# An attention and two MLPs on one core: the first weights' splits ranked among the second attention's units, and half of the fifth block's result moved out of the buffer rings

## The chip, the cores and the metric

The kernel runs on one core of a Trainium2 chip. The metric is the time of one execution on the device in microseconds (us). Three runs of the kernel before gave a median of 1018.32 us (1017.8 to 1019.97).

## What is computed

A block-causal attention (4 batches, 8 heads, 576 positions, 64 values per head; a position sees all positions of its own block of 64 and of the blocks before), whose output, 2304 tokens by 512, goes through two multilayer perceptrons of the same size:

```python
def _attn_ref(q, k, v):
    scores = scale * np.matmul(q, k.transpose(0, 1, 3, 2))
    mask = block_i >= block_j
    scores = np.where(mask, scores, -1000000000.0)
    scores = scores - np.max(scores, axis=-1, keepdims=True)
    attn = np.exp(scores)
    attn = attn / (np.sum(attn, axis=-1, keepdims=True) + 1e-09)
    return np.matmul(attn, v)

def _moe_ref(x, w_in, w_out):      # 512 -> 2048 -> 512
    h = x @ w_in
    g = np.maximum(0.01 * h, h)
    return g @ w_out

def _moe2_ref(x, w_in, w_out):     # 512 -> 2048 -> 512
    h = x @ w_in
    g = h * (1.0 / (1.0 + np.exp(-h)))
    return g @ w_out
```

All inputs and outputs are 4-byte floats; the weights reach the kernel as 8-byte floats and are converted on the chip.

## The kernel before, in words

The tokens are cut into six blocks of 384. The attention of block b+1 is computed while the first MLP of block b runs, so that TensorE always has matmuls of the MLP to do. The second MLP follows, in nine blocks of 256 tokens, each in pairs of hidden chunks, and its first weights are converted and split during the last layer blocks.

**One layer block** has 16 steps f (NF), one for each 128 of the 2048 hidden units: a first half H (h, into PSUM; L1114 in block 0, L1119 to L1121 later), the gate (leaky relu, ScalarE, L1167), and a second half A that adds to four chunks of PSUM, acc (L1131 in block 0, L1139 later). In the text, H31 is the first half of step 31, counted over all blocks: block 0 has steps 0 to 15, block 1 has 16 to 31, and so on. Block 0 takes the weights as plain 4-byte floats (4 matmuls per half). From block 1 on each factor is split in a high and a low part of the faster type fp32r, and three products are added (12 matmuls per half). For that each first weight is split once: ScalarE copies the high part (L296, w<-wx) and VectorE or GpSimd subtracts it to get the low one (L312, w<-wx,w). Likewise the gate's result is split at each step into ghi (L296) and glo (L312).

**The attention** is made of units (one head, 128 queries or some tails): scores s (TensorE, L833 or L838), the row maximum (VectorE, L845 or L847), the exponential p (ScalarE, L855), the norm (L862 to L865), the high part hl (L869) and the low part (VectorE, L874), a transposing DMA pt<-hl (L882), the value products x (TensorE, L896 to L898), and the output's way out of PSUM: a half by ScalarE (L721), the sum by VectorE (L727), and a split into xhi and xlo.

**What sets the order.** Nothing is ordered by hand. The class Schedule is a list scheduler that runs while the program is built: each piece of work is a task with the engines that may do it (and a cost in ns on each), the tasks it depends on, and a rank. An engine that comes free in the planner's own clock takes the ready task of lowest rank, and the tasks are written out on each engine in that order; on the chip, each engine then runs its list as it stands. A layer step has rank 16 blk + f; work that TensorE waits for is put ahead by GATE (−1000) or SHORT (−500). The conversion of the first weights (convert(), L326) ranks from 10.5 on, the units of attention 1 from 11 on, those of attention 2 some 75 to 92, the splits of the first weights (split_weights(), L401) as below:

```python
ts = split(DM, lambda d=d: d["x"], parts, deps, step_of(1, f) - LEAD + i % 2, ...)   # L423
```

With LEAD 2.0 that is 14 + f. From f = 5 on, a split's result lies in space that the keys and queries of attention 1 use until its last scores are done, so these splits depend on all of them.

convert() turns 8-byte floats into 4-byte ones: a load (SP, L337), a copy scaled by ScalarE into a buffer cy (L344), the low words into a buffer cc by ScalarE (L352) or VectorE (L354), a sign (VectorE, L357), a shift (VectorE, L361) and a sum (L366, VectorE or GpSimd). The loads land in the ring wraw. The same three rings of buffers, wraw, cy and cc, also take the results of the layer blocks: when the last second half of a block is done, its four chunks of acc are copied out of PSUM (ScalarE L296 or VectorE L298, y<-acc) and stored to memory (yT<-y, SP, L1226). Which ring each chunk takes is set for each block by YRINGS ("r" wraw, "y" cy, "c" cc, "w" a place among the second weights):

```python
YRINGS = ("ryry", "crcr", "crcr", "crcr", "cycy", "wwww")
```

A buffer that holds a chunk comes free when its store has landed. The second MLP's weights are split into tiles of a pool "late" (LATE tiles, L1245), which takes the place of the attention's buffers when the attention has ended, and the planner adds the weights that don't fit as earlier steps come free.

Of the kernel before, what the change touches and what calls it, by code (L numbers as in the profile page):

```python
# [19 lines left out]
P = 128  # L20
# [6 lines left out]
NB2 = 256  # L27
FAST = 5
SEQ = 576
LATE = 10  # L30
NATIVE = 15
WARM = 11
LEAD = 2.0
LOAD0 = -1000
TURN = 0
COLD = 1.2
# [4 lines left out]
START0, START1 = -42.0, -26.0  # L41
STEP2 = 1.2
W2_BEFORE, W2_FIRST, W2_SECOND = 6, 30, 32
YRINGS = ("ryry", "crcr", "crcr", "crcr", "cycy", "wwww")
W2_AHEAD = 22
KQR, KR, QR, VR = 960, 1728, 2048, 1792
PR, HLR, PTR = 1408, 2304, 2304
# [165 lines left out]
def attn_mlp_mlp(  # L213
# [50 lines left out]
    def act(n, psum=False, pointers=0):  # L264
        return 0.833 * n + (52 if psum else 94) + 93 * pointers
# [7 lines left out]
    def dve2x(n, pointers=0):  # L273
        return Both(0.521 * n + 68 + 61 * pointers)

    def pool(n):
        return Both(2.35 * n + 100)
# [48 lines left out]
    def convert(src, f, sl, rk, load_rank, to=None):  # L326

        d = {}  # L330
        raw_free, raw_after, raw_users = raws.next()
        cy_free, cy_after, cy_users = cys.next()
        cc_free, cc_after, cc_users = ccs.next()

        def load():
            r = raw.tile([P, DM], I64, tag="wraw", name="wraw")
            nc.sync.dma_start(out=r, in_=src[f, :, sl])  # L337
            d["w0"] = r.bitcast(U32).rearrange("p (n two) -> p n two", two=2)[:, :, 0]
            d["sign"] = r.bitcast(U16).rearrange("p (n four) -> p n four", four=4)[:, :, 3]
            d["top"] = r.bitcast(F32).rearrange("p (n two) -> p n two", two=2)[:, :, 1]  # L340

        def scaled(e):
            d["y"] = cy.tile([P, DM], F32, tag="cy", name="cy")
            nc.scalar.activation(d["y"], d["top"], AF.Copy, scale=2.0**-112)  # L344

        def half_words(i):
            return d["c"].bitcast(U16).rearrange("p (n two) -> p n two", two=2)[:, :, i]

        def low(e):
            d["c"] = cc.tile([P, DM], U32, tag="cc", name="cc")  # L350
            if e == "ACT":
                nc.scalar.activation(half_words(0), d["w0"], AF.Copy, scale=2.0**-29)  # L352
            else:
                nc.vector.tensor_scalar(half_words(0), d["w0"], 2.0**-29, None, op0=ALU.mult)  # L354

        def signed(e):
            nc.vector.tensor_scalar(half_words(1), d["sign"], 0x8000, None, op0=ALU.bitwise_and)  # L357

        def shifted(e):
            yu = d["y"].bitcast(U32)  # L360
            nc.vector.tensor_scalar(yu, yu, 3, None, op0=ALU.logical_shift_left)  # L361

        def added(e):
            ci = d["c"].bitcast(I32)
            d["x"] = d["c"].bitcast(F32) if to is None else to
            engine[e].tensor_tensor(d["x"].bitcast(I32), d["y"].bitcast(I32), ci, op=ALU.add)  # L366

        t_load = dma(raw_free, load_rank, DM * P * 8, load, after=raw_after)
        raws.takers.append(t_load.issue)
        t_y = plan.add({"ACT": act(DM)}, [t_load, *cy_free], rk, scaled, cy_after)  # L370
        cys.takers.append(t_y)
        t_w = plan.add({"DVE": dve2x(DM), "ACT": act(DM)}, [t_load, *cc_free], rk, low, cc_after)
        ccs.takers.append(t_w)
        t_c = plan.add({"DVE": dve2x(DM)}, [t_load], rk, signed, [t_w])
        t_t = plan.add({"DVE": dve2x(DM)}, [t_y], rk, shifted)
        t_x = plan.add(on_vector(DM), [t_w, t_c, t_t], rk, added)
        raw_users += [t_y, t_w, t_c]
        cy_users.append(t_x)
        if to is not None:
            cc_users.append(t_x)  # L380
        return d, t_x, cc_users
# [808 lines left out]
    def add_second(s):  # L1190
# [10 lines left out]
        y_there[blk] = []  # L1201
        for c in range(NC):
            kind = YRINGS[blk][c]
            if kind == "w":
                free, after, users = (), (), []
            else:
                turns = {"r": raws, "c": ccs, "y": cys}[kind]
                free, after, users = turns.next()
            d = {}

            def evac(e, c=c, d=d, kind=kind):
                if kind == "w":
                    if c % 2 == 0:
                        late_y.append(slot1(F32, "yl"))
                    y = late_y[-1][:, c % 2 * DM : (c % 2 + 1) * DM]
                elif kind == "r":
                    y = raw.tile([P, DM], I64, tag="wraw", name="y").bitcast(F32)
                elif kind == "c":
                    y = cc.tile([P, DM], U32, tag="cc", name="y").bitcast(F32)
                else:  # L1220
                    y = cy.tile([P, DM], F32, tag="cy", name="y")
                d["y"] = y[:, :n]
                copy(e, d["y"], s.acc[c][:, :n])
# [1 line left out]
            def store(c=c, d=d):  # L1225
                nc.sync.dma_start(out=yT[blk][:, c, :], in_=d["y"])  # L1226

            if kind == "w":
                after = y_order[-1:]
            t = plan.add(copy_on(n, True), [s.t_g2, *free], GATE + rk, evac, after)  # L1230
            if kind == "w":
                y_order.append(t)
            else:
                turns.takers.append(t)
# [427 lines left out]
```

## Time and profile before

| what | before |
|---|---|
| median of 3 runs | 1018.32 us (1017.8 to 1019.97) |
| profiled execution, its own time | 1017.75 us |
| profiled execution, its span | 1016.0 us |
| TensorE (PE) busy | 981.6 us |
| VectorE (DVE) busy | 762.7 us |
| ScalarE (ACT) busy | 577.2 us |
| GpSimd (POOL) busy | 196.3 us |
| mean granted TensorE clock | 0.992 |

The span is from the first to the last instruction of the profiled execution; its own time is 1.75 us more. PE is TensorE's matmuls, PEld its weight loads, which run beside them, SP the engine that issues the DMAs. The granted clock has two levels, 2.4 GHz (1.00) and 1.2 GHz (0.50); a mean between them says how much of a stretch had which.

### The profile page before, as it was taken

Reading aid. Unit: us, or ns where it says so; the run is one execution under the profiler, and the core shown is the slowest. Engines: PE = TensorE matmul, PEld = TensorE weight load, DVE = VectorE, ACT = ScalarE, POOL = GpSimd, SP = SyncE. Lnnn points to the kernel's source line nnn. Section 1 sums busy time; section 2 is a strip of 40 time slices with the busy share of each in tenths; the row PEclk is TensorE's granted clock in tenths of the full one; section 3 lists DMA queues with packets and bytes.
Section 4 is the critical chain, followed back from the end, with each engine's and each line's share of the span. In section 5 each row is a group of like instructions: output and inputs, shape, how many; then the busy total and the mean of one; then the engine's idle time right before and its main releaser. Section 6 shows DMA issues by size and latency. Waiting matters only on the chain.

```text
span 1016.0 us, 18148 instructions
## 1 busy us (share of the span) xinstructions
PE 981.6 (97%) x6417; PEld 862.8 (85%) x6417; DVE 762.7 (75%) x1891; ACT 577.2 (57%) x1398; POOL 196.3 (19%) x287
## 2 busy tenths in 40 slices
PE   7899999999899999999999999999999999999998
PEld 4656557999799999999999898888989889898897
DVE  6888879687978878877647999976666667666564
ACT  5886768676667666666545668643333333333332
POOL 3173438112130114112203124510000000000000
PEclk9999999999799999999999999999999999999999
DMA  8757772565664656568434445410010100000000
GB/s 266 247 148 179 193 146 71 116 147 111 143 143 117 132 134 123 114 138 191 112 62 135 145 146 176 125 43 22 22 42 1 43 1 22 22 1 22 1 22 22
DMA packets 159451, 102.64 MB, mean 101 GB/s; under 512 B 131456, under 2 KB 143744, under 8 KB 159360
## 3 DMA queue, kind: packets, MB, share of 16 engines
q1 hardware_dynamic: 159360, 101.48, 39.6%
q8 instruction: 50, 0.82, 0.3%
q14 instruction: 41, 0.34, 0.1%
HBM read 67.37 MB, written 9.44 MB: 76 GB/s over the span
## 4 chain that ended last, share of the span: by engine, by line
PE 51%; DVE 3%; DMA 2%; ACT 1%; issue 1%; POOL 0%; SPq 0%; DVEq 0%; POOLq 0%; ACTq 0%
PE h L1332 13%; PE acc L1455 11%; PE acc L1471 7%; PE h L1333 6%; PE acc L1139 6%; PE h L1119 2%; PE h L1121 2%; PE h L1120 2%; PE s L838 1%; DMA wraw<-w 1%; DMA yT<-y 1%; DMA pt<-hl 1%; PE x L896 0%; DMA kqr<-kq_l 0%; PE x L898 0%
## 5 line engine op out<-in xcount | busy, mean ns | idle before, releaser
L1139 PE MATMUL acc<-ghi,w 128*128 128x384 f32 x640 | 164.2, 337 | 1.9 <-ACT ghi L296 1.2
L1344 ACT ACTIVATE xlo<-xlo 128x256 f32<-128x256 f32 x144 | 59.6, 414 | 139.1 <-DVE xlo L1341 139.0
L1332 PE MATMUL h<-xhi,w 128*128 128x512 f32 x352 | 132.0, 398 | 0.0
L1341 DVE TENSOR_REDUCE xlo<-h 128x256 f32<-128x512 f32 x144 | 99.3, 690 | 37.1 <-PE h L1333 34.8
L1139 PEld LDWEIGHTS acc<-ghi,w 128*128 128x128 f32 x640 | 114.0, 188 | 3.3 <-ACT ghi L296 1.5
L1119 PE MATMUL h<-xhi,w 128*128 128x384 f32 x320 | 109.7, 343 | 0.3 <-ACT g L1167 0.3
L1120 PE MATMUL h<-xlo,w 128*128 128x384 f32 x320 | 107.6, 336 | 0.0
L1139 PE MATMUL acc<-glo,w 128*128 128x384 f32 x320 | 107.4, 336 | 0.2 <-DVE glo L312 0.2
L1121 PE MATMUL h<-xhi,w 128*128 128x384 f32 x320 | 107.5, 336 | 0.0
L855 ACT ACTIVATE p<-s,st 128x288 f32<-128x288 f32 (+5 forms) x144 | 73.4, 512 | 47.9 <-DVE st L847 35.2
L1333 PE MATMUL h<-xhi,w 128*128 128x256 f32 x352 | 98.9, 281 | 0.0
L312 DVE TENSOR_TENSOR g<-xlo,xhi 128x256 fp32r<-128x256 f32 x136 | 61.4, 452 | 40.0 <-ACT xhi L296 39.6
L874 DVE SCALAR_TENSOR_TENSOR hl<-p,st,hl 128x576 f16<-128x576 f32 (+6 forms) x120 | 80.4, 674 | 14.5 <-ACT hl L869 11.5
L296 ACT ACTIVATE xhi<-xlo 128x256 fp32r<-128x256 f32 x144 | 59.0, 415 | 48.8 <-PE acc L1455 29.1
L1332 PE MATMUL h<-xlo,w 128*128 128x512 f32 x224 | 85.5, 398 | 0.0
L869 ACT ACTIVATE hl<-p,st 128x576 f16<-128x576 f32 (+7 forms) x111 | 65.8, 596 | 25.9 <-DVE st L865 7.2
L896 PE MATMUL x<-pt,v 128*128 128x128 f16 (+1 forms) x432 | 70.7, 214 | 9.4 <-DMA pt<-hl 4.1
L1332 PEld LDWEIGHTS h<-xhi,w 128*128 128x128 f32 x352 | 66.3, 188 | 13.7
L1167 ACT ACTIVATE g<-h 128x384 f32<-128x384 f32 x96 | 46.6, 485 | 48.1 <-PE h L1121 44.8
L897 PE MATMUL x<-pt,v 128*128 128x128 f16 (+1 forms) x432 | 68.6, 212 | 0.0
L1471 PE MATMUL acc<-w,xhi 128*128 128x512 f32 (+1 forms) x225 | 67.5, 384 | 0.0
L1333 PEld LDWEIGHTS h<-xhi,w 128*128 128x128 f32 x352 | 66.6, 189 | 1.0
(147 smaller groups left out, 2514.4 us busy)
## 6 DMA issues: line engine op xcount, KB each, us to landing
wraw<-w SPq DMA_DIRECT2D x64, 512.0 KB, 4.5
kqr<-kq_l SPq DMA_DIRECT2D x16, 480.0 KB, 4.0
v<-vL SPq DMA_DIRECT2D x32, 160.0 KB, 3.5
out<-o SPq DMA_DIRECT2D x18, 256.0 KB, 2.0
yT<-y SPq DMA_DIRECT2D x20, 192.0 KB, 2.3
kqr<-kq_l SPq DMA_DIRECT2D x8, 416.0 KB, 3.5
kqr<-kq_l SPq DMA_DIRECT2D x8, 384.0 KB, 3.5
yr<-yT SPq DMA_DIRECT2D x6, 512.0 KB, 4.0
```

Source lines behind the costliest of these rows:

```text
L855: nc.scalar.activation(p[:rows, k0:k1], u.s[i][:rows, :w], AF.Exp, bias=nm[:rows], accum_out=s2[:rows, i : i + 1])
L874: nc.vector.scalar_tensor_tensor(hl[:rows, 1, :n], p[:rows], rc[:rows], hl[:rows, 0, :n], op0=ALU.mult, op1=ALU.subtract)
L896: nc.tensor.matmul(g.x[:, o], a, hi, start=j == 0, stop=False)
L1119: nc.tensor.matmul(h, w1_lo[s.f][:, sl], hi[:, c, : s.n], start=c == 0, stop=False)
L1120: nc.tensor.matmul(h, w1_hi[s.f][:, sl], lo[:, c, : s.n], start=False, stop=False)
L1121: nc.tensor.matmul(h, w1_hi[s.f][:, sl], hi[:, c, : s.n], start=False, stop=c == NC - 1)
L1139: nc.tensor.matmul(s.acc[c][:, : s.n], a, b, start=s.f == 0 and i == 0, stop=s.f == NF - 1 and i == 2)
L1332: nc.tensor.matmul(o, whi[:, sl], x, start=c == 0, stop=end, skip_group_check=True)
L1333: nc.tensor.matmul(o[:, :NB2], wlo[:, sl], x[:, :NB2], start=False, stop=end, skip_group_check=True)
L1341: nc.vector.tensor_reduce(place(2 * j, 2), both, axis=AX.X, op=ALU.add)
L1455: nc.tensor.matmul(o, a, b, start=bank not in seen, stop=end and j == 2, skip_group_check=True)
L1471: nc.tensor.matmul(o[:, c], a, b[:, c], start=False, stop=end, skip_group_check=True)
```

## The change

Four things are edited. The splits of the first weights rank 16 + f + 55 (+ 0 or 1) in place of 16 + f − 2, that is 71 + f and up. The planner's costs of the five operations of convert() are raised by 50 to 150 ns, and the sum's entry gets a cost of its own for VectorE. Chunks 0 and 1 of the fifth block's result (block 4) go to a new tile "y4" of the pool late, that is free from the end of the attention on, rather than to a buffer of cc and of cy; chunks 2 and 3 stay in cc and cy. The pool late has nine tiles for weights rather than ten.

```diff
-LATE = 10
+LATE = 9
...
-LEAD = 2.0
+LEAD = -55.0
...
-YRINGS = ("ryry", "crcr", "crcr", "crcr", "cycy", "wwww")
+YRINGS = ("ryry", "crcr", "crcr", "crcr", "llcy", "wwww")
...
-        t_y = plan.add({"ACT": act(DM)}, [t_load, *cy_free], rk, scaled, cy_after)
+        t_y = plan.add({"ACT": act(DM) + 50}, [t_load, *cy_free], rk, scaled, cy_after)
...
-        t_w = plan.add({"DVE": dve2x(DM), "ACT": act(DM)}, [t_load, *cc_free], rk, low, cc_after)
+        t_w = plan.add({"DVE": dve2x(DM) + 110, "ACT": act(DM) + 150}, [t_load, *cc_free], rk, low, cc_after)
...
-        t_c = plan.add({"DVE": dve2x(DM)}, [t_load], rk, signed, [t_w])
-        t_t = plan.add({"DVE": dve2x(DM)}, [t_y], rk, shifted)
-        t_x = plan.add(on_vector(DM), [t_w, t_c, t_t], rk, added)
+        t_c = plan.add({"DVE": dve2x(DM) + 110}, [t_load], rk, signed, [t_w])
+        t_t = plan.add({"DVE": dve2x(DM) + 60}, [t_y], rk, shifted)
+        t_x = plan.add({"DVE": dve(DM) + 70, "POOL": pool(DM)}, [t_w, t_c, t_t], rk, added)
...
-            if kind == "w":
-                free, after, users = (), (), []
+            if kind in "lw":
+                free, after, users = [end_of_attention] if kind == "l" else (), (), []
...
+                if kind == "l":
+                    if c % 2 == 0:
+                        late_y.append(late().tile([P, 2 * DM], F32, tag="y4", name="y4", bufs=1))
+                if kind in "lw":
                     y = late_y[-1][:, c % 2 * DM : (c % 2 + 1) * DM]
```

Since the planner decides the order, the whole order moves, on all engines. Three places follow.

The first is ScalarE in the last steps of layer block 0. `w<-wx` are copies for the first weights' splits; `g<-h` is the gate of a layer step, `k<-kqr` and `q<-kqr` belong to heads of attention 2, `p,st<-s,st` is an exponential, `hl<-p,st` a high part, `x<-x` a half of the attention's output on its way out. Before:

```order
L296 ACTIVATE w<-wx 128x512 x2
L1167 ACTIVATE g<-h 128x384
L296 ACTIVATE w<-wx 128x512 x3
L721 ACTIVATE x_1684<-x 64x128 x2
L296 ACTIVATE w<-wx 128x512 x3
L721 ACTIVATE x_1684<-x 64x64 x2
L296 ACTIVATE k<-kqr 128x576
L855 ACTIVATE p,st<-s,st 128x320
L296 ACTIVATE w<-wx 128x512
L296 ACTIVATE xhi<-x_1684 128x192
L1167 ACTIVATE g<-h 128x384
L296 ACTIVATE w<-wx 128x512 x3
```

After:

```order
L721 ACTIVATE x_1675<-x 64x128 x2
L869 ACTIVATE hl<-p,st 128x320
L855 ACTIVATE p,st<-s,st 128x448
L296 ACTIVATE w<-wx 128x512 x2
L721 ACTIVATE x_1675<-x 64x64 x2
L665 ACTIVATE q<-kqr 128x384
L296 ACTIVATE w<-wx 128x512
L296 ACTIVATE xhi<-x_1675 128x192
L869 ACTIVATE hl<-p,st 128x448
L296 ACTIVATE w<-wx 128x512
L855 ACTIVATE p,st<-s,st 128x288 x2
L1167 ACTIVATE g<-h 128x384
```

The copies for the splits now stand in ones and twos among work of attention 2, where it was twos and threes with one key and one exponential among them.

The second is TensorE at the turn from layer block 1 to 2, between A30 and H32. Before, 128 rows of attention stand there without a layer half; this is a piece of them, the end of one unit's values, three scores, and the start of the next values:

```order
L896 MATMUL x<-pt,v 128x64
L897 LDWEIGHTS v
L897 MATMUL x<-pt,v 128x64
L898 LDWEIGHTS v
L898 MATMUL x<-pt,v 128x64
L838 MATMUL s<-k,q 128x256 x2
L838 MATMUL s<-k,q 128x384 x2
L838 MATMUL s<-k,q 128x128 x2
L896 LDWEIGHTS v
L896 MATMUL x<-pt,v 128x128
```

After, the end of the attention between H31 and A30, A30 itself, and the first of the values behind it:

```order
L898 LDWEIGHTS v
L898 MATMUL x<-pt,v 128x128
L838 MATMUL s<-k,q 128x384 x2
L1139 MATMUL acc<-ghi,w 128x384 x2
L1139 MATMUL acc<-glo,w 128x384
L1139 MATMUL acc<-ghi,w 128x384 x2
L1139 MATMUL acc<-glo,w 128x384
L1139 MATMUL acc<-ghi,w 128x384 x2
L1139 MATMUL acc<-glo,w 128x384
L1139 MATMUL acc<-ghi,w 128x384 x2
L1139 MATMUL acc<-glo,w 128x384
L896 LDWEIGHTS v
```

Between two layer halves there is now one part of a unit's values and a score or two. Counted over the whole order, the first scores of attention 2 moved from behind H18 to behind H14.

The third is ScalarE at the turn from layer block 4 to 5; `y<-acc` is a chunk of the fifth block's result, `cy<-wraw` the first step of a conversion, `w<-cc` a copy for a split of the second weights. Before:

```order
L296 ACTIVATE y<-acc 128x384 x2
L1167 ACTIVATE g<-h 128x384
L296 ACTIVATE y<-acc 128x384
L296 ACTIVATE ghi<-g 128x384
L344 ACTIVATE cy<-wraw 128x512 x2
L1167 ACTIVATE g<-h 128x384
L296 ACTIVATE w_6700<-cc 128x512
L296 ACTIVATE ghi<-g 128x384
```

After:

```order
L296 ACTIVATE ghi<-g 128x384
L296 ACTIVATE y_6692<-acc 128x384 x2
L296 ACTIVATE y<-acc 128x384
L344 ACTIVATE cy<-wraw 128x512
L1167 ACTIVATE g<-h 128x384
L296 ACTIVATE ghi<-g 128x384
L344 ACTIVATE cy<-wraw 128x512
L1167 ACTIVATE g<-h 128x384
L296 ACTIVATE ghi<-g 128x384
L296 ACTIVATE w_6604<-cc 128x512
```

The first two chunks go to the new tile, all three of ScalarE's chunks stand behind one gate, and ghi comes ahead of the copy for a split.

## Rows read from the trace of the kernel before

**Rows 1.** First page: busy time by engine; busy tenths and clock in 40 slices.

```profile
PE 981.6 (97%) x6417; PEld 862.8 (85%) x6417; DVE 762.7 (75%) x1891; ACT 577.2 (57%) x1398; POOL 196.3 (19%) x287
...
PEclk9999999999799999999999999999999999999999
```

**Rows 2.** Busy time by stretch: us, engines' busy us (instructions), PEclk, DMA share, GB/s.

```profile
0.00:52.00 52.00, 40.09 (x207) 26.06 (x208) 39.26 (x120) 35.78 (x97) 14.25 (x23) 0.93 0.76 256
...
130.00:165.00 35.00, 33.36 (x184) 20.46 (x183) 28.30 (x69) 27.13 (x66) 16.90 (x22) 1.00 0.60 108
165.00:185.00 20.00, 20.00 (x106) 17.86 (x105) 15.64 (x23) 12.25 (x30) 13.10 (x14) 1.00 0.33 88
...
255.00:290.00 35.00, 29.69 (x216) 26.79 (x215) 29.85 (x97) 23.61 (x67) 8.46 (x17) 0.85 0.71 157
290.00:540.00 250.00, 243.79 (x1880) 233.58 (x1880) 187.30 (x527) 159.19 (x408) 49.32 (x99) 1.00 0.57 124
540.00:568.00 28.00, 25.61 (x141) 23.96 (x140) 21.71 (x42) 16.79 (x33) 6.00 (x4) 1.00 0.43 136
...
616.50:640.00 23.50, 22.18 (x144) 20.07 (x143) 21.19 (x40) 18.55 (x39) 14.15 (x16) 1.00 0.47 156
640.00:660.00 20.00, 19.84 (x123) 17.56 (x121) 18.26 (x28) 12.52 (x29) 12.92 (x13) 1.00 0.45 132
```

The engines of these rows are PE, PEld, DVE, ACT and POOL, in this order.

**Rows 3.** The same table, finer, at the turn from block 1 to 2.

```profile
255.00:263.00 8.00, 5.22 (x46) 4.47 (x45) 6.79 (x24) 5.37 (x15) 0.91 (x4) 1.00 0.83 158
263.00:273.00 10.00, 8.14 (x53) 7.12 (x50) 9.30 (x30) 6.07 (x17) 1.81 (x4) 0.50 0.62 132
```

**Rows 4.** TensorE's waits, 255 to 290 us: total us, times, longest.

```profile
PE s L838 <- ACT p L855: 2.9, 4, 1.6
PE x L896 <- DMA pt<-hl: 1.3, 2, 0.8
PE x L896 <- DVE x L727: 1.1, 2, 0.7
```

**Rows 5.** Value products of L896 by stretch: PE and PEld busy (instructions), PEclk.

```profile
130.00:161.00 31.00, 3.71 (x26) 2.42 (x26) 1.00 0.66 119
161.00:184.80 23.80, 0.45 (x4) 0.37 (x4) 1.00 0.30 78
...
255.00:271.40 16.40, 4.94 (x20) 2.52 (x20) 0.74 0.72 145
```

**Rows 6.** First weights' splits: ScalarE 150 to 168 us, GpSimd in all; ns min/median/max.

```profile
L296 ACT ACTIVATE w<-wx x20: 613/621/631, 152.0 to 167.0; 128x512 fp32r<-128x512 f32 x20
...
L312 POOL TENSOR_TENSOR w<-wx,w x20: 1265/1494/1786, 56.0 to 170.1; 128x512 fp32r<-128x512 f32 x20
```

**Rows 7.** TensorE in order of time, one half step each; the second from the chain.

```profile
158.95 2.74 PE L1131 MATMUL acc<-g,wx 128*128 128x384 f32 x8
...
568.71 2.08 PE acc L1139 x12
```

**Rows 8.** VectorE's low parts and TensorE's value products behind them: start, us.

```profile
155.32 0.41 DVE L874 SCALAR_TENSOR_TENSOR hl<-p,st,hl 128x192 f16<-128x192 f32 x1
...
161.61 0.19 PE L896 MATMUL x<-pt,v 128*128 128x64 f16 x1
...
176.86 0.54 DVE L874 SCALAR_TENSOR_TENSOR hl<-p,st,hl 128x320 f16<-128x320 f32 x1
...
184.90 0.23 PE L896 MATMUL x<-pt,v 128*128 128x128 f16 x1
...
259.72 0.69 DVE L874 SCALAR_TENSOR_TENSOR hl<-p,st,hl 128x448 f16<-128x448 f32 x1 [0.23 <-ACT hl L869]
...
263.89 0.26 PE L896 MATMUL x<-pt,v 128*128 128x128 f16 x1 [0.79 <-DMA pt<-hl]
```

**Rows 9.** VectorE's waits, 110 to 165 us.

```profile
DVE x L727 <- ACT x L721: 1.9, 3, 1.1
```

**Rows 10.** Turn from block 4 to 5: TensorE's waits, the chain, ScalarE's timeline.

```profile
PE acc L1139 <- ACT ghi L296: 1.2, 1, 1.2
PE acc L1139 <- DVE y L298: 0.7, 1, 0.7
...
551.85 6.05 DMA yT<-y
...
557.49 0.67 ACT L344 ACTIVATE cy<-wraw 128x512 f32<-128x512 f32 x1 [3.79 <-DMA yT<-y]
```

**Rows 11.** TensorE's longest wait, 616.5 to 660 us; VectorE's g subtractions, ns.

```profile
PE acc L1455 <- DVE glo L312: 0.9, 2, 0.4
...
L312 DVE TENSOR_TENSOR g<-xlo,xhi x136: 417/425/1493, 632.9 to 1010.0; 128x256 fp32r<-128x256 f32 x136
```

**Rows 12.** TensorE's longest wait, 0 to 52 us.

```profile
PE pt L1053 <- DVE spare L1047: 4.6, 3, 2.1
```

More of the change, by code (lines that the diff above doesn't have):

```diff
@@ L1226, in store @@
                 nc.sync.dma_start(out=yT[blk][:, c, :], in_=d["y"])
-            if kind == "w":
+            if kind in "lw":
                 after = y_order[-1:]
             t = plan.add(copy_on(n, True), [s.t_g2, *free], GATE + rk, evac, after)
-            if kind == "w":
+            if kind in "lw":
                 y_order.append(t)
```

## The prediction

> **What bounds the kernel now.** I read the profile from the outside in. The first page [rows 1] shows TensorE busy in 97% of the span and VectorE in 75%; of the forty clock digits one alone is low, the twelfth. So a change that doesn't remove matmuls can win only TensorE's idle time, 1016.0 − 981.6 = 34 us, and the time in which it runs at a lower clock. The table of stretches [rows 2] tells where these are: of 35 us from 255 to 290 TensorE was busy in 29.69, at a mean clock of 0.85; from 130 to 165, 290 to 540 and 540 to 568 it lacked 1.6, 6.2 and 2.4 us, at full clock, and the rest of the 34 us lies mostly at the start (11.9 in the first 52 us, where the attention of block 0 is computed with nothing else to do). The worst place is thus the turn from layer block 1 to 2. The finer table [rows 3] splits it: first 2.8 us of idle in 8 at clock 1.00, then ten microseconds at 0.50, the lower of the two levels (1.2 of 2.4 GHz). The list of TensorE's waits [rows 4] names what it waits for there: exponentials, DMA transposes and the sum of x, which are three links of the attention of block 2.
>
> Why is the attention late at that place and nowhere else as much? The value products (L896) by stretch [rows 5] answer: attention 1 runs until about 161 us, then there are 4 products of that line in 24 us, and the backlog is asked for in a bunch of 20 in 16 us. In the pause ScalarE makes 20 copies for the first weights' splits, of 0.62 us each, between 152.0 and 167.6 [rows 6]. They rank as 14 + f, ahead of everything of the second attention (ranks of 63 and more), so the planner empties them in one go.
>
> **The order at that turn (A).** In the new order the splits rank 71 + f, and the bunch of values between A30 and H32 is gone: no more than one part of a unit's values stands between two layer halves. I take it that this turn then looks like other turns of the kernel, with about 1 us of idle time. The stretch now loses 35 − 29.69 = 5.3 us idle, and half of the 8.14 us [rows 3] in which TensorE was busy at half clock, 4.1 us. Together 9.4; less the 1.0 that stays: **−8.4 us**. The ends are −9.4 (nothing waits) and, where the cause is not the bunch, 0.
>
> **What is asked for earlier (B).** The price is that attention 1 and 2 stand earlier among the layer steps. Counted in TensorE's work (matmuls of the new order by the durations of the trace; a half step of block 0 is 2.7 us, one of a later block 2.08 [rows 7]), the last values of attention 1 stand one whole step of block 0 earlier, 5.2 us, and values of attention 2 from 12.5 to 22 us earlier. VectorE's own work ahead of the last low part (L874) is 1 to 2.5 us more for attention 1, since some splits now stand ahead of it, and 4 to 8 us less for attention 2. How much room is there? From the end of L874 to the first product are 161.61 − 155.73 = 5.9 us for the last unit of attention 1, and 184.90 − 177.40 = 7.5 for the first of attention 2; where TensorE really waited for the transpose it was 263.89 − 260.41 = 3.5 [rows 8]. So attention 1 has 2.4 us in hand against 5.2 + 1 to 2.5 asked: 3.8 to 5.3 us of wait, if VectorE has no free time to give. It has: it is busy in 28.30 of 35 and 15.64 of 20 us in 130 to 185 [rows 2], 11 us idle. For attention 2 this gives 4 to 8 us less work, 11 idle and 4 in hand, 19 to 23, against the 12.5 to 22 that are asked: just enough. Ends 0 and +5.3; since part of VectorE's idle time is itself waits, of 1.9 us for ScalarE's half of x alone before 165 us [rows 9], I take the middle, **+2.5 us**, at full clock.
>
> At full clock, because 2.4 us of waits between 540 and 568 left the granted clock at 1.00, while 2.8 us of them before 263 were followed by 0.50 [rows 2, 3]: rows of both kinds exist, and the smaller loss is the nearer one. The Trainium skill has a rule against this change here: "TensorE: Matmul & The Clock Gate", section "A second HAM failure mode: psum-queue depth-cycling", says that an array which idles briefly but often between groups of matmuls swings between its two clock levels and pays for it between the bursts. By it the new wait would cost another 4.1 us, and the sum would be −3.5 instead of −7.6; the trace agrees at 263 and not at 540.
>
> The splits are as many as before: 30 copies on ScalarE, and 8 subtractions on VectorE and 22 on GpSimd in place of 10 and 20. In the trace GpSimd's take 1.49 us in the median [rows 6], and nothing but first layer steps of block 1 waits for them; each copy of f from 5 on stands at least seven steps ahead of the first layer step that reads it, in the old order and the new. Nothing.
>
> **The fifth block's result (C).** At the turn from layer block 4 to 5 TensorE lacks 2.4 us [rows 2]; 1.2 of it are a wait for ScalarE's ghi and 0.7 one for VectorE's copy of a chunk of y [rows 10]. The chain explains the first: the stores of y take 6.05 us to land, and ScalarE's copy of the next weights into the buffer that held y (L344) waits 3.79 us for them, with ghi behind it on the same engine [rows 10]. With chunks 0 and 1 in a tile of their own, only one buffer of each ring waits for a store, and in the new order ghi stands ahead of the split copies. The VectorE copy's 0.7 stays partly, as one of the four copies of y is still VectorE's: **−1.7 us** (ends −2.4 and 0). The tile is paid for with one late weight tile less; middle splits of the second weights come about one step (4.2 us) later, where they have 25 us and more in hand. Nothing, unless that cover is wrong.
>
> **Start of the second MLP (D).** From 616.5 to 660 VectorE is busy in 39.45 of 43.5 us [rows 2]. The new costs in convert() make the planner move work between engines there: one more weight subtraction goes to GpSimd, and four of its eight g subtractions come to VectorE (L312, 0.43 us each in the median [rows 11]) with low parts and copies of x. Priced by form, VectorE has 4.2 us more work ahead of the sums of the first eight pairs. Its idle time there is 4.1 us, and TensorE already waits 0.9 us for VectorE's glo [rows 11]. Ends 0 and +4.2, I take a quarter: **+1.0 us**, as most of it fits the idle time.
>
> **The start (E).** ScalarE's work ahead of the first gate falls by 1.8 us in the new order, and VectorE's is unchanged; TensorE waits longest for VectorE there, 4.6 us [rows 12]. **−1.0 us**, between −2 and +1. **Blocks 3 to 5 (F)** are reordered everywhere by the shifted plan without a pattern that I can price; 6.2 us are idle there now: 0, between −3 and +3.
>
> Sum: −8.4 + 2.5 − 1.7 + 1.0 − 1.0 = −7.6 us. The profiled execution took 1017.75 us (span 1016.0); the median of the runs is 0.57 above it. So 1010.15 + 0.57 = **1010.7 us**.
>
> **The rivals.** *Nothing new waits.* VectorE's 11 idle us are filled, D fits: A −9.4, C −2.4, E −1.8, so 1004.1 + 0.6 = 1004.7; with F at its low end 1001.7. For it speaks that 19 to 23 us cover 12.5 to 22. Chance 0.20. *The stall moves, and the clock falls there.* The wait of B is 2.5 to 5.3 us in several short pieces, and the half clock of [rows 3] comes with it at 150 to 185 us: 4.1 to 6.9 us on top of the sum, 1014.8 to 1017.6. For it speaks that the waits before 263 were no longer than these. Chance 0.17. *Slower: the backlog stands at the turn of block 0.* Matmuls stand in one order, so a product that isn't ready holds the layer steps behind it. If VectorE's free time can't be used, because its idle pieces stand behind waits for ScalarE, units of attention 2 that are asked 22 us earlier get only 8 us from less work and 4 in hand: a wait of 10 us, and 4.1 for the clock, in place of 2.5. That is 1010.15 + 11.6 + 0.57 = 1022.3. It decides from a wait of about 10 us at 145 to 200 us (2.5 + 7.6) on; against it speaks that ScalarE now has its splits in pairs and no longer blocks. Chance 0.10. *It doesn't do what it says*: the bunch is not the cause but the speed of attention 2 itself, and the same 9.4 us are lost over the next steps: 1016 to 1019. Chance 0.05.
>
> **How the numbers follow.** My own sum has 0.48, with bounds of 1005 to 1014. About 0.2% is what a measurement of this kernel can tell from no change, here 1016.3 to 1020.3. Faster takes the sum, the first rival and most of the second, 0.80; the same takes the end of the second, half of the fourth and a piece of the third, 0.10; slower 0.10. The range takes in the first rival to its low end, 1001.5, and the second, 1017.6; it leaves out the third and half of the fourth.
>
> **What would show it.** In the changed profile the copies of w<-wx should begin some 5 to 8 us earlier and lie among exponentials of attention 2, in pairs; the twelfth clock digit should be 9; 255 to 290 should lack about 1 us. If B is right, TensorE's waits for transposes or for x at 140 to 185 us sum to 2 or 3 us; if they exceed 5, or a clock digit of slices 5 to 8 is low, the second or third rival holds. At the turn from block 4 to 5, L344 should no longer wait for yT<-y, nor ghi delay a second layer. From 616 to 660, waits for glo of over 2 us would make D too small. The forecast is wrong if the half clock stays, at whatever place.

## The result, and the profile after

The changed kernel takes **1004.5 us** in the median (four runs, 1001.75 to 1006.81), the kernel before beside it 1019.1 (1017.8 to 1021.46): a ratio of 0.9854, 95% interval 0.9827 to 0.9881. That is 14.6 us less; the prediction said 1010.7, 7.6 less than the 1018.3 it started from. The time is inside the range and almost at the first rival (nothing new waits, 1004.7), but that is chance: new waits came, and other terms were larger. The profiled execution took 1004.43 us (span 1002.7).

The first page, as in [rows 1]:

```profile
PE 973.1 (97%) x6417; PEld 857.6 (86%) x6417; DVE 767.6 (77%) x1901; ACT 576.5 (57%) x1394; POOL 191.2 (19%) x281
...
PEclk9999999999999999999999999999999999999999
```

The low clock digit is gone, and TensorE is busy 8.5 us less with as many matmuls. The stretches that answer to [rows 2], each begun earlier by what the program is ahead there, and first, for comparison, the one stretch of the kernel before that [rows 2] leave out:

```profile
52.00:130.00 78.00, 76.17 (x404) 45.60 (x405) 66.30 (x171) 57.29 (x138) 37.82 (x42) 1.00 0.70 177
```

```profile
0.00:50.00 50.00, 40.67 (x215) 26.43 (x216) 39.51 (x120) 37.00 (x99) 13.31 (x23) 0.97 0.75 251
50.00:128.00 78.00, 71.98 (x405) 42.73 (x405) 72.43 (x182) 60.56 (x146) 35.46 (x42) 1.00 0.80 199
128.00:163.00 35.00, 33.02 (x179) 20.75 (x177) 31.13 (x76) 26.04 (x66) 20.53 (x25) 1.00 0.38 87
163.00:183.00 20.00, 20.00 (x124) 16.28 (x120) 18.26 (x35) 13.74 (x31) 13.26 (x15) 1.00 0.65 150
...
253.00:288.00 35.00, 35.00 (x271) 33.15 (x269) 31.14 (x97) 27.58 (x76) 5.59 (x14) 1.00 0.66 149
288.00:535.00 247.00, 238.73 (x1841) 229.09 (x1840) 185.43 (x521) 160.28 (x402) 45.02 (x91) 1.00 0.58 126
535.00:560.00 25.00, 25.00 (x147) 25.00 (x146) 17.52 (x34) 13.61 (x27) 3.33 (x3) 1.00 0.40 133
...
610.00:633.00 23.00, 22.77 (x154) 20.73 (x153) 21.74 (x40) 14.91 (x32) 17.25 (x18) 1.00 0.37 121
```

The turn from block 1 to 2 lacks nothing at all, at full clock; so does the turn from block 4 to 5. In exchange 50 to 128 us lacks 6.0 us, where 52 to 130 lacked 1.8 before. The value products (L896) of the changed kernel by stretch, to be held against [rows 5], show that the pause is gone: 15 products where there were 4. In the 16 us before H32 there are 22, about as many as the 20 of before, but without a wait.

```profile
130.00:161.00 31.00, 3.28 (x24) 2.22 (x24) 1.00 0.36 75
161.00:183.00 22.00, 2.64 (x15) 1.47 (x15) 1.00 0.59 137
183.00:247.00 64.00, 11.57 (x66) 6.45 (x66) 1.00 0.63 120
247.00:263.00 16.00, 3.85 (x22) 2.05 (x21) 1.00 0.67 139
```

Idle time and a lower clock are easier to hold together in one number, which I call the **delay** of a stretch: the time from the start of each matmul to the start of the next, less the median of that for the same line and shape in the profiles of before and of the changed kernel, summed over the matmuls of the stretch. Attention that is moved from one stretch to another doesn't enter it. Stretches are cut where the first matmul of a step starts.

| delay, us | before | changed | difference | the prediction's term |
|---|---|---|---|---|
| start to H0 | 16.3 | 11.8 | −4.6 | E −1.0 |
| H0 to H16 (block 0) | 7.5 | 12.4 | +4.9 | B +2.5 |
| H16 to H40 (the turn 1 to 2) | 13.8 | 2.6 | −11.2 | A −8.4 |
| H40 to H80 | 12.3 | 14.5 | +2.2 | F 0 |
| H80 to the second MLP | 3.9 | 0.1 | −3.9 | C −1.7 |
| its first 8 pairs (16 hidden chunks) | 2.4 | 0.8 | −1.6 | D +1.0 |
| the rest | −0.2 | 0.6 | +0.8 | |
| sum | 56.0 | 42.7 | −13.3 | −7.6 |

The sum is the whole difference of the two spans, 1016.0 − 1002.7 = 13.3. The +0.8 of the last but one row stands in the two pairs right behind the first eight. One expectation below (LATE 9) speaks of 16 pairs where these 8 are meant.

How far one profile can be trusted shows in kernels that are run below and are written in the same order up to the turn from block 4 to 5: two besides the kernel before (the tile alone, LATE 9 alone), and three besides the changed one (itself again, and without the tile at LATE 10 and 9). The first three have 15.1 to 17.8 us at the start, 7.5 to 9.2 in block 0, 13.2 to 13.8 at the turn and 11.1 to 12.3 from H40 to H80; the other four 9.4 to 14.1, 12.4 to 13.4, 2.6 to 3.2 and 12.2 to 14.5. So the turn and block 0 stand far outside the scatter, the start less far, and H40 to H80 hardly.

The new waits of block 0 stand not where the prediction looked, at 140 to 185 us, but earlier. TensorE's waits in the changed kernel from 52 to 100 us:

```profile
PE x L896 <- DMA pt<-hl: 3.2, 2, 2.4
PE x L896 <- ACT cy L344: 1.5, 1, 1.5
PE x L896 <- DVE x L727: 0.5, 1, 0.5
```

The longest is 2.42 us, up to 67.28. SP's timeline before it:

```profile
56.46 5.94 SPq L337 DMA_DIRECT2D wraw<-w  x2
63.16 1.67 SPq L882 DMA_TRANSPOSE pt<-hl  x1
```

ScalarE's and VectorE's:

```profile
58.08 0.76 ACT L869 ACTIVATE hl<-p,st 128x576 f16<-128x576 f32 x1
...
58.46 1.53 DVE L354 TENSOR_SCALAR cc<-wraw 128x512 uint16<-128x512 uint32 x1
59.88 1.75 DVE L366 CUSTOM_DVE_ANT_0 wx<-cy,cc 128x1024 uint16<-128x1024 uint16 x1
61.55 0.45 DVE L357 TENSOR_SCALAR cc<-wraw 128x512 uint16<-128x512 uint16 x1
...
62.22 0.81 DVE L874 SCALAR_TENSOR_TENSOR hl<-p,st,hl 128x576 f16<-128x576 f32 x1
63.04 0.11 DVE L845 MEMSET s<- 64x64 f32 x1
```

The high part hl is ready at 58.84. The low part, which needs it, comes at 62.22, since VectorE has four pieces of a weight's conversion ahead of it, and the transpose is issued right behind the low part (62.22 + 0.81). Two of these pieces took 1.53 and 1.75 us where others of the same lines take 0.44 and 0.67 in this stretch, 2.2 us more together. So the longest wait is of the kind that term B was about (attention behind VectorE's work), with conversions ahead of it and not splits. GpSimd had a subtraction (L312) running beside both long pieces. In block 0 of the changed kernel 12 of 67 conversion pieces on VectorE took over 1 us, before 5 of 57; in block 0 of every kernel here GpSimd was busy beside each such long piece, for two thirds of its time or more. That alone doesn't make the delay of block 0: with LEAD alone 11 of 54 pieces are as long, and the delay is 5.5 us.

### The profile page after: what moved, and what is told of

Same layout as the page of the kernel before. It is cut to its first block, busy times and chain, and to the rows that moved or that the text cites. A ratio compares the mean times of both kernels' runs of the same rounds, so it can differ in the third digit from the quotient of the medians.

```text
span 1002.7 us, 18167 instructions
## 1 busy us (share of the span) xinstructions
PE 973.1 (97%) x6417; PEld 857.6 (86%) x6417; DVE 767.6 (77%) x1901; ACT 576.5 (57%) x1394; POOL 191.2 (19%) x281
## 4 chain that ended last, share of the span: by engine, by line
PE 53%; DVE 3%; DMA 2%; ACT 1%; issue 1%; SPq 0%; DVEq 0%; ACTq 0%
PE h L1336 13%; PE acc L1459 11%; PE acc L1475 7%; PE acc L1139 7%; PE h L1337 6%; PE h L1119 2%; PE h L1121 2%; PE h L1120 2%; DMA pt<-hl 1%; PE s L838 1%; DMA wraw<-w 1%; DMA kqr<-kq_l 1%; DVE xlo L1345 0%; PE x L896 0%; DVE xlo L312 0%
## 5 line engine op out<-in xcount | busy, mean ns | idle before, releaser
L874 DVE SCALAR_TENSOR_TENSOR hl<-p,st,hl 128x576 f16<-128x576 f32 (+6 forms) x120 | 86.6, 730 | 15.4 <-ACT hl L869 12.4
L312 DVE TENSOR_TENSOR g<-xlo,xhi 128x256 fp32r<-128x256 f32 x140 | 64.0, 457 | 38.5 <-ACT xhi L296 38.1
L869 ACT ACTIVATE hl<-p,st 128x576 f16<-128x576 f32 (+7 forms) x116 | 68.6, 597 | 28.5 <-DVE st L865 9.9
L896 PE MATMUL x<-pt,v 128*128 128x128 f16 (+1 forms) x432 | 69.1, 211 | 13.4 <-DMA pt<-hl 6.6
L1336 PEld LDWEIGHTS h<-xhi,w 128*128 128x128 f32 x352 | 66.3, 188 | 13.7
L897 PE MATMUL x<-pt,v 128*128 128x128 f16 (+1 forms) x432 | 66.9, 209 | 0.0
```

What stands on the lines that cost most here:

```text
L874: nc.vector.scalar_tensor_tensor(hl[:rows, 1, :n], p[:rows], rc[:rows], hl[:rows, 0, :n], op0=ALU.mult, op1=ALU.subtract)
L896: nc.tensor.matmul(g.x[:, o], a, hi, start=j == 0, stop=False)
L1336: nc.tensor.matmul(o, whi[:, sl], x, start=c == 0, stop=end, skip_group_check=True)
```

## The experiments

The bunch is counted here as the matmuls of L896 to L898 that the written order has between H31 and H32 (the 128 rows of the section on the change begin at A30 and hold scores and weight loads too). Before it is 72, in the changed kernel 18. It doesn't come from one edit: LEAD −55 alone gives 96, the costs alone 81, and only the two together 18. So each edit was run alone first.

**LEAD alone.** The kernel before with

```diff
-LEAD = 2.0
+LEAD = -55.0
```

> The kernel before with LEAD -55 alone. In its order the value products still pause from step 16 to 20, and the bunch before H32 is larger (96 products rows of the six hundred, against 72 before). Theory (the loss at the turn of block 1 to 2 is the bunch, and the rank alone does not remove it): the half clock and 4 to 8 us of idle time before H32 stay; median 1016 to 1022 us, the turn's stretch (H16 to H40) 150 us or longer as before. Rival (the prediction's working: the rank of the splits removes the loss): the stretch falls to about 140 us and the median to 1008 to 1011.

Measured: 1019.5 us, ratio 1.0007 (0.9991 to 1.0023), H16 to H40 158.8 us with a delay of 19.4. Busy time and clock of this kernel in stretches of 10 us:

```profile
255.00:265.00 10.00, 5.87 (x45) 4.52 (x42) 8.15 (x25) 5.95 (x16) 1.97 (x6) 0.73 0.55 116
265.00:275.00 10.00, 7.61 (x49) 6.27 (x49) 9.45 (x33) 6.59 (x22) 1.03 (x2) 0.50 0.64 135
275.00:285.00 10.00, 9.92 (x66) 9.29 (x67) 7.66 (x28) 6.69 (x19) 1.70 (x4) 0.74 0.57 125
```

The rank alone moves nothing away: idle time and the half clock are both there, and last longer than in [rows 3] (20.5 us at 0.50 at this turn, 10.2 before). Nor does it spread the splits: 18 of ScalarE's copies still run between 154.4 and 170.4 us, in the changed kernel 20 between 146.6 and 170.9. The rival, which is the prediction's own main step, falls.

**The costs alone.** The kernel before with the five changed lines of convert().

> The kernel before with the new costs in convert() alone. In its order the start is that of the changed kernel up to the first layer steps, the pause of the value products is there, and 81 products stand between H31 and H32. Theory (start from the costs, turn from both together): H0 begins at 47 to 49 us as in the changed kernel (52.0 before), the half clock before H32 stays; median 1013 to 1017. Rival 1 (the costs alone remove the turn's loss): median 1004 to 1008. Rival 2 (the earlier start of the changed kernel is not in the order but differs from run to run): H0 at 50 to 53 us, median 1017 to 1021.

Measured: 1021.2 us, ratio 1.0027 (1.0006 to 1.0048). H0 at 48.0, as expected, the turn's delay 19.6; the median lies above the theory's and above the kernel before, since block 0's delay rose to 16.7, which the theory had left out. The start's gain is the costs', and alone it is more than eaten up.

**The tile alone.** The kernel before with LATE 9, "llcy" and the code for kind "l".

> The kernel before with the fifth block's first two chunks in the new tile and LATE 9, old LEAD and costs. Its order is that of before up to the turn of block 4 to 5. Theory: the 2.4 us of idle time between H80 and the second MLP go, and with them 1.5 us that overlapping records hide; median 1015 to 1017.5, block 5 (H80 to the second MLP) 66 to 68.5 us in place of 70.4. Rival (the copies for the second weights, one step later, give it back at the start of the second MLP): block 5 as in the theory, but waits of 2 us or more for glo or ghi behind it, median 1018 to 1021.

Measured: 1022.9 us, ratio 1.0032 (1.0017 to 1.0048): slower, and above the theory's range and the rival's. Block 5 took 69.5 us (before 70.4), against 66 to 68.5 expected, and the first 8 pairs of the second MLP have a delay of 6.3 us (2.4 before). ScalarE at the turn from block 4 to 5, and TensorE's waits from 616 to 700 us (code lines behind L1215 stand 4 later in this kernel):

```profile
554.63 0.52 ACT L296 ACTIVATE ghi<-g 128x384 fp32r<-128x384 f32 x1
555.04 0.66 ACT L344 ACTIVATE cy<-wraw 128x512 f32<-128x512 f32 x1
560.52 0.68 ACT L344 ACTIVATE cy<-wraw 128x512 f32<-128x512 f32 x1 [4.82 <-DMA yT<-y]
```

```profile
PE h L1337 <- POOL w L312: 1.9, 2, 1.2
PE acc L1475 <- POOL w L312: 1.4, 1, 1.4
```

One chunk still sits in a buffer of cy, and ScalarE waits for its store as before, now 4.82 us. In the second MLP TensorE waits 3.3 us for low parts of the second weights on GpSimd, for which it didn't wait before: the rival's loss, but for w and not for glo or ghi.

**LEAD and costs without the tile.** The changed kernel with

```diff
-LATE = 9
+LATE = 10
-YRINGS = (..., "llcy", "wwww")
+YRINGS = (..., "cycy", "wwww")
```

> The changed kernel with the fifth block's result in the rings as before and LATE 10: LEAD and costs alone. Its order is that of the changed kernel up to the turn of block 4 to 5. Theory: all but the 2.4 to 3.9 us of that turn is kept: median 1006.5 to 1009; H40 at 306 to 309 us, clock 1.00 from 255 to 290. Rival (the new tile is worth nothing, or the turn's waits were those of the old plan): median 1003.5 to 1005.5.

Measured: 1005.9 us, ratio 0.9867 (0.9834 to 0.9900), between the theory's range and the rival's. Block 5 took 66.56 us, the same as in the changed kernel, and its delay is 0.1. ScalarE waits here 0.84 us for a store, behind ghi:

```profile
544.88 0.53 ACT L296 ACTIVATE ghi<-g 128x384 fp32r<-128x384 f32 x1
545.31 0.65 ACT L344 ACTIVATE cy<-wraw 128x512 f32<-128x512 f32 x1
546.80 0.69 ACT L344 ACTIVATE cy<-wraw 128x512 f32<-128x512 f32 x1 [0.84 <-DMA yT<-y]
```

So the gain of the turn from block 4 to 5 belongs to the new plan and not to the tile. ScalarE's order doesn't tell the two apart: with the tile alone, too, three chunks are copied out behind one gate, and ghi stands ahead of L344 (554.63 and 555.04 above). The stores do. SP with the tile alone, and then here:

```profile
545.91 7.01 SPq L337 DMA_DIRECT2D wraw<-w  x3
553.01 2.32 SPq L1230 DMA_DIRECT2D yT<-y  x4
```

```profile
538.44 0.33 SPq L337 DMA_DIRECT2D wraw<-w  x1
541.65 2.83 SPq L1230 DMA_DIRECT2D yT<-y  x4
```

With the tile alone the four stores follow right behind weight loads and land 5.9 to 6.0 us after they are issued. Here one load went out 3.2 us ahead, and the stores land after 2.0 to 2.8 us. That the loads ahead of the stores make the difference is my reading; it was not tried by itself.

The next four are all the changed kernel with one thing altered, to have bunches of four sizes.

**LEAD −54**, one less than the change's (36 rows).

> The changed kernel with LEAD -54 in place of -55. In its order 36 rows of value products of L896 to L898 stand between H31 and H32 (18 with -55, 72 in the kernel before, 96 with -55 alone). Theory (the loss at the turn grows with the bunch: 2.7, 13.5, 19.5 us of delay for 18, 72 and 81 to 96 rows): 5 to 7 us of delay from H16 to H40, median 1007 to 1009. Rival 1 (all or nothing: no loss as long as the clock does not fall): H16 to H40 within 1 us of the changed kernel's delay, median 1003.5 to 1006. Rival 2 (any plan but the chosen one loses the gain): median 1013 or more.

Measured: 1014.9 us (five runs, 1006.94 to 1015.63), ratio 0.9936 (0.9904 to 0.9968). The turn's delay is 8.0 us (5 to 7 expected) at a clock of 1.00 throughout. The first rival falls: this turn costs more also where the clock stays. Of the 8.0 us, 1.7 lie in the step from H31 to H32 itself (0.1 in the changed kernel) and 2.0 only at step 39.

```profile
265.00:275.00 10.00, 7.69 (x66) 6.99 (x64) 8.98 (x27) 7.62 (x21) 2.14 (x5) 1.00 0.75 151
```

The profiled execution has a span of 1010.8 us. The median was expected at 1007 to 1009; what is over lies mostly in block 0, which the theory had left out (delay 18.3 for 12.4, with 10.2 us of it at half clock). The median is that of the second rival, 1013 or more; that any other plan loses the gain doesn't hold, as the rule for three pairs below shows.

**LEAD −80**, behind the whole second attention (72 rows).

> The changed kernel with LEAD -80: the splits rank behind the whole second attention; 72 rows stand between H31 and H32, as in the kernel before, with the start and the last layer blocks planned at the changed kernel's costs. Theory (bunch): 12 to 15 us of delay from H16 to H40, the half clock before H32 is back, median 1013 to 1017. Rival (a rank among or behind the attention's units is what counts, and the bunch is a side effect): median 1004 to 1007.

Measured: 1015.7 us, ratio 0.9977 (0.9956 to 0.9997); delay of the turn 13.3, with 13.7 us at half clock. A rank behind the attention's units doesn't do it either.

**The planner's rule on GpSimd.** The planner keeps VectorE's and GpSimd's tasks apart in time if their costs are of the class Both. Both + 110 is a plain float in Python: the change thus also took convert()'s tasks on VectorE out of that rule. Two kernels part the two effects. In the first the numbers are the old ones and the rule is dropped (60 rows), as in

```diff
-        t_c = plan.add({"DVE": dve2x(DM) + 110}, [t_load], rk, signed, [t_w])
+        t_c = plan.add({"DVE": dve2x(DM) + 0}, [t_load], rk, signed, [t_w])
```

> The changed kernel with the old numbers for the operations of convert(), but plain ones, which the planner does not keep apart from GpSimd's (the new costs are plain numbers too: adding to a Both gives a plain number). 60 rows stand between H31 and H32; the start has an order of its own. Theory: 9 to 12 us of delay from H16 to H40; if the earlier H0 came from dropping the port's rule, H0 is at 47 to 49 us, if it came from the higher costs, at 51 to 54. Median 1010 to 1016. Rival (bunch of no matter): 1003 to 1007.

Measured: 1017.7 us, ratio 0.9986 (0.9976 to 0.9996), above the expected range; H0 at 51.3, the turn's delay 8.0 where 9 to 12 were expected, block 0's 16.4. In the second the numbers are the new ones and the rule is kept (108 rows), as in

```diff
-        t_c = plan.add({"DVE": dve2x(DM) + 110}, [t_load], rk, signed, [t_w])
+        t_c = plan.add({"DVE": Both(dve2x(DM) + 110)}, [t_load], rk, signed, [t_w])
```

> The changed kernel with the new numbers for the operations of convert(), kept apart from GpSimd's as before. 108 rows stand between H31 and H32, the most of all. Theory: 20 us of delay or more from H16 to H40, with the half clock; if the earlier H0 came from the higher costs, H0 is at 47 to 49 us, if from dropping the port's rule, at 51 to 54. Median 1019 to 1027. Rival (bunch of no matter): 1003 to 1008.

Measured: 1031.7 us, ratio 1.0124 (1.0095 to 1.0152), above the expected range; H0 at 47.5, block 0's delay 7.3, the turn's 24.9 us, that of the second MLP's first 8 pairs 11.0, and 5.9 more in the two behind them. Its worst stretch:

```profile
255.00:265.00 10.00, 4.38 (x26) 3.21 (x26) 7.35 (x26) 5.47 (x17) 3.04 (x7) 0.61 0.60 145
265.00:275.00 10.00, 8.24 (x61) 7.18 (x59) 8.49 (x33) 6.70 (x20) 1.56 (x2) 0.50 0.57 123
```

The earlier H0 comes with the higher numbers, not with dropping the rule. The bunch goes the other way. With LEAD −55 all four cases are here: 96 rows with the old numbers and the rule, 108 with the new ones and the rule, 60 with the old ones without it, 18 with the new ones without it. So dropping the rule shrinks the bunch with either set of numbers, and the raised numbers shrink it only where the rule is dropped, though the edit is written as a change of numbers alone.

**What the tile and LATE are worth.** Three kernels on one chip: before with LATE 9; the changed one with the rings of before, but LATE 9; the changed one itself again.

> The kernel before with LATE 9 alone (one late weight tile less, no tile for y). Its order is that of before up to the turn of block 4 to 5. Theory (what made the kernel with tile and LATE 9 slower was the missing weight tile, since the copies for the second weights come later): 2 to 4 us of more waits in the first 16 pairs of the second MLP, as there, median 1020 to 1023. Rival (the new tile's own plan, with the splits shifted by the new place of y, made it slower): within 1 us of before, 1018 to 1020.

> The changed kernel with the fifth block's result in the rings as before, but LATE 9. Theory (the tile itself is worth nothing at the turn of block 4 to 5 in the new plan, since four copies behind one gate and ghi ahead of the splits already hide the stores): block 5 at 66.6 us as with and without it, median within 2 us of the changed kernel's 1004.5. Rival (tile and LATE each count): 1007 or more.

> The changed kernel itself beside these. Theory: 1003 to 1006; the kernel without the new tile took 1005.9, and if that difference is real, this is again at least 1 us faster than that.

Measured: 1018.7 us (ratio 0.9988, 0.9971 to 1.0005), 1006.1 (0.9857, 0.9829 to 0.9884) and 1006.0 (0.9857, 0.9832 to 0.9882). The missing weight tile isn't what made the tile alone slower, since LATE 9 alone is as fast as before; the plan around the new tile is. And the changed kernel with and without the tile can't be told apart: 1004.5 and 1006.0 with it, 1005.9 and 1006.1 without.

**A try to beat both.** Kernels that kept convert() under the planner's rule had 5.5 to 9.2 us of delay in block 0, those without it 12.4 to 18.3. So the rule was kept for the first three pairs only, where the bunch stays at 18 rows, by four costs of this form:

```diff
-        t_c = plan.add({"DVE": dve2x(DM) + 110}, [t_load], rk, signed, [t_w])
+        t_c = plan.add({"DVE": (Both if src is w1 and f < 3 else float)(dve2x(DM) + 110)}, [t_load], rk, signed, [t_w])
```

> The changed kernel, with the operations of convert() for the first three pairs of first weights (f below 3) kept apart from GpSimd's in the plan as before, at the new numbers. 18 rows stand between H31 and H32 as in the changed kernel, and attention 1 is 12 rows of value products further at step 8. Theory (dropping the port's rule costs block 0 some 5 us of delay, since the kernels with it have 5.5 to 9.2 us there and those without 12.4 to 18.3): block 0 (H0 to H16) with 8 to 11 us of delay, the turn at 2.6 to 3.2, median 1000 to 1004. Rival (in block 0 the place of the work counts and not the rule): 12 us or more of delay in block 0, median 1004 to 1008.

Measured: 1005.7 us, ratio 0.9884 (0.9856 to 0.9912); block 0's delay 15.3. The rival holds: no gain over the change. What keeps block 0's delay low in the kernels with the whole rule stays open.

Put in order of the bunch, all profiles: the delay of the turn (H16 to H40), and of the one step in which the bunch stands (H31 to H32):

| rows between H31 and H32 | kernel | delay of the turn, us | of the step, us |
|---|---|---|---|
| 18 | changed; again; no tile; no tile, LATE 9; rule for three pairs | 2.6; 3.2; 2.8; 2.6; 4.1 | 0.1 in each |
| 36 | LEAD −54 | 8.0 | 1.7 |
| 60 | old numbers, rule dropped | 8.0 | 4.6 |
| 72 | before; tile alone; LATE 9 alone; LEAD −80 | 13.8; 13.2; 13.8; 13.3 | 8.7; 8.5; 8.6; 8.7 |
| 81 | costs alone | 19.6 | 13.5 |
| 96 | LEAD alone | 19.4 | 14.1 |
| 108 | new numbers, rule kept | 24.9 | 19.2 |

The kernels differ in start, costs, rank, tile and rule. The delay of the step rises with the bunch at each of the seven sizes and goes by none of these; that of the turn does so too, but for two pairs of neighbours that are alike. What makes the bunch is how many units of attention 2 are left when layer block 1 has run out, and this goes in the main with the pause: between H16 and H20, 9 rows of values are placed before, with LEAD alone and with the new numbers and the rule, 21 with the costs alone, 27 with LEAD −80, 36 with LEAD −54, 48 with the old numbers without the rule and 60 in the changed kernel. It isn't the pause alone: 9 rows there go with bunches of 72, 96 and 108.

## Why the prediction was right, and where it was wrong

In short: the loss sat where the prediction said and went with the bunch. Which edit removes the bunch it had wrong, and most of the other terms it had wrong in size or in cause.

**A** was right in its mechanism and in where the time is: the loss at the turn from block 1 to 2 is a bunch of attention behind a pause, about half waits and half the lower clock. Its size was short by 2.8 us. The prediction counted the 5.3 us idle [rows 2] and 4.1 of half clock [rows 3] and kept 1.0 for what "other turns" have; the idle time left is 0, and the delay fell by 11.2, of which 8.6 lie in the step from H31 to H32. That is the 9.4 that were counted, and 1.8 beside it, which I put down to matmuls that start late without a gap that the list of waits would show. The step that failed is its cause: "in the new order the splits rank 71 + f, and the bunch … is gone" put the rank first. The prediction read the bunch off the new order, so that it is gone was no luck; what removes it the prediction only argued, and the rank alone makes it 96 rows and a delay of 19.4 us. By the planner's code a rank picks only among tasks that are ready; with LEAD −80 the splits rank behind every unit, and 72 rows are there all the same, with a pause of 27 rows between H16 and H20 in place of 9. I read this as units of attention 2 that aren't ready when the splits are; what makes them ready earlier in the changed plan was not tried by itself. Rank, raised numbers and dropped rule together make 18 rows, one step of LEAD either way 36 (run) or 60 (counted in the order, not run): it is a good plan that was found, not a rule.

**B** had the right sign, +4.9 for +2.5, and lay within its ends of 0 and 5.3, in part by luck, since the place was wrong: most of the waits stand at 57 to 90 us, the longest behind conversions, and the kernel with LEAD alone has less delay in block 0 than before (5.5 for 7.5). It is the edit of the costs that brings it (16.7 alone), and in it rather the dropped rule than the numbers: 16.4 with the old numbers without the rule, 7.3 with the new ones and the rule. The wait of 155.1 us, 1.2 us long, is all that came where the prediction looked.

**C** was wrong in its cause. The stores' wait was to go because two chunks leave the rings; with the tile alone ScalarE still waits 4.82 us, and without the tile the changed plan has the same 66.56 us for block 5. The other reason in the same sentence, "ghi stands ahead of the split copies", doesn't hold either: with the tile alone ghi stands ahead of the copy, too (at 561.61 and 564.05), and TensorE's gain is 0.9 us of delay in place of 3.9. What goes with the gain is that the stores of y land within 2.0 to 3.4 us (changed kernel, with and without the tile), where they took 5.9 to 6.0 with the tile alone. The size, −1.7, was short of −3.9: all 2.4 us of idle time went, and 1.5 of late starts beside it.

**D** had the wrong sign: 4.2 us more work on VectorE, priced by form, ahead of the sums of the first eight pairs gave no wait at all; the delay fell by 1.6, of which 0.8 came back in the two pairs behind. The changed kernel with the rings of before has 2.9 in the first eight, so this seems a matter of which pieces come when, and not of VectorE's sum. **E** was mis-sized: −4.6 for −1.0, outside its ends. The prediction counted ScalarE's work ahead of the first gate, 1.8 us less, and not the order in which the start's transposes follow each other: TensorE waited 4.6 us for VectorE there [rows 12], and in the changed kernel the row of that wait, and the one that is now the longest of the start, read

```profile
PE s L1020 <- DVE cy L361: 4.3, 1, 4.3
...
PE pt L1053 <- DVE spare L1047: 1.0, 2, 0.7
```

The wait for the first scores (L1020) was there before, too:

```profile
PE s L1020 <- DMA spare<-kq: 3.0, 1, 3.0
```

The start also has 3.4 us less at half clock in these two profiles. Some of E is chance: the second profile of the changed kernel has 14.1 us of delay at its start and 6.8 us at half clock, as many as before, which makes E −2.2. The sign is not: in all nine profiles with the new numbers H0 starts at 45.1 to 49.8 us, in the five with the old ones at 50.8 to 53.5. **F**, taken as 0 with ends of 3, was +2.2, hardly more than such profiles differ by.

So the forecast's 7.6 us were six terms of which four were too cautious (A, C, D, E: 21.3 us gained for 10.1 forecast) and two too kind (B, F: 7.1 lost for 2.5); 0.8 lost behind the first eight pairs were in no term. That the waits of block 0 would pull the clock down, the second rival, did not happen in the profiled execution of the changed kernel: 8.0 us of them from H0 to H16, and 1.00 throughout. But its second profile has 3.4 us at 0.50 just behind H0, and the kernels with LEAD −54 and −80 have 10.2 and 6.8 us in the same stretch, so it can. The rule of the Trainium skill that the prediction set against the change ("TensorE: Matmul & The Clock Gate", "A second HAM failure mode: psum-queue depth-cycling") agrees with those and not with the changed kernel's first profile. The third rival did not come either: no wait in block 0 after 128 us was longer than 1.2 us.

## What to carry to other kernels

Where a planner writes the order, read a loss in the written order first: count what stands in a row between two steps that must not wait, and see by each edit alone whether that count moves, before any of it is put down to the edit whose name fits. A planner's rank picks only among tasks that are ready, and its costs have a part in when they are. When a number type carries a rule (here Both), arithmetic on it can drop the rule unseen; here the raised numbers with the rule kept made the kernel slower than before (1031.7 us).

## What the runs showed of the hardware

The start of one and the same kernel is not the same from run to run: H0 of the changed kernel began at 47.5 us in one profile and at 49.8 in another, which is most of the spread of its span (1002.7 and 1005.1). And the lower clock doesn't go by the sum of idle time: 2.8 us of short waits before 263 us were followed by it in the kernel before [rows 3], 2.3 us in one stretch of LEAD −54 were not (7.69 of 10 busy, at 1.00), and 8.0 us spread over block 0 of the changed kernel were not in one profile. In another, with 6.7 us of waits there, 3.4 us ran at 0.50.
